# Two 8-block DMA transposes into two rings instead of one 16-block transpose into one ring, in a chunked linear-attention kernel with two feed-forward layers

## The chip, the cores and the metric

The program runs on one core of a Trainium2 chip. The metric is device time of one execution in microseconds (us); lower is better. Engines in the text: PE (TensorE, matrix products), DVE (VectorE), ACT (ScalarE), POOL (GpSimd) and SP (SyncE, which here only issues DMAs). Each engine works through its own list of instructions in order.

## The reference

A recurrent attention runs over 768 time steps for 4 batches of 8 heads, head size 40; its output goes through two feed-forward layers, the first with h·cos(h), the second with h·clip(h+3, 0, 6)/6.

```python
for t in range(S):                       # S = 768, state is (B, H, D, D), D = 40
    y[:, :, t] = einsum('bhd,bhde->bhe', r_t, state)
    Sa = einsum('bhde,bhe->bhd', state, a_t)
    state = state * w_t[:, :, None, :] - einsum('bhd,bhe->bhde', Sa, b_t)
    state = state + einsum('bhd,bhe->bhde', v_t, k_t)
x = y reshaped to (3072, 320)
h = x @ w_in;  x = (h * cos(h)) @ w_out                  # 320 -> 2048 -> 320
h = x @ w_in2; x = (h * clip(h + 3, 0, 6) / 6) @ w_out2
```

## The kernel before, in words

The 768 steps are cut into 12 chunks of 64 steps. A *unit* is one chunk of one batch (8 heads): 48 units, numbered n = 4·chunk + batch. Each unit's work comes in two parts.

*Preparation*, which doesn't need the state. `pA` loads the rows of a, r, b and k (tile `raw`) and the decays (`pip`). `pB` multiplies them and writes the k/b rows and the a/r rows as fp16 (the halves `KBss` and `ARss` of the tile `AKs`, two buffers in turn). `pT` turns both by a DMA transpose issued by SP. `pC` multiplies the turned rows on PE (tile `p`, 8 matmuls), masks the product on DVE (`LN`) and stores it for the inverse. For each chunk, `iL` to `iE` invert the triangular matrices of all four units; `iB` is a chain of 62 short DVE instructions (`tmp`, `Tt`).

*The recurrence*, in the order of the chunks: `cU` (PE products with the state, `uh`), `cA`, a transpose `FT` of the rows `FS`, `cG` (`gm`, `GF`), and `cF`, which ends the unit with the output `xy` and the new state. It reads the turned a/r rows (`ART`) up to its end.

The feed-forward work of a chunk is 8 *groups* a layer (`mA`, `mB`), 192 groups in all. A group is 16 PE matmuls into `h`, one ACT function and one DVE instruction that make `s`, a rounded copy `ghl` of `s` by ACT or DVE, the rest of the rounding by DVE (`ghl<-s,ghl`), and 12 matmuls into `acc`. `h` and `s` have two buffers each, `ghl` three.

No order is written by hand. Each operation is recorded by `Plan.rec` (from L156) with an assumed cost, and `Plan.order` (L244) lists them for the engines by 50 passes of a priority schedule over these costs and the data dependencies. An operation recorded as `either` goes to DVE, or for a copy to DVE or ACT, whichever the schedule finds free. So one edited operation, cost or buffer can move any instruction of any engine. The emitted instructions all carry the lines of `emit` (L452, L456), so the rows below go by tile.

The turned rows lie in `AKT` (L556), nine slots of 8 blocks. Unit n takes two neighbouring slots, n mod 8 and the one behind it (L846): a/r rows first, k/b rows second. Slot n mod 8 + 1 still holds the a/r rows of unit n-7, so the transpose of unit n waits for `cF` of unit n-7, and for `pC` of unit n-1, whose k/b rows are in the first slot.

Of the kernel before, what the change touches and what calls it, by code (L numbers as in the profile page):

```python
# [9 lines left out]
F16 = mybir.dt.float16  # L10
# [9 lines left out]
B, H, S, D = 4, 8, 768, 40  # L20
# [66 lines left out]
class Plan:  # L87
# [68 lines left out]
    def rec(self, attr, eng, name, a, kw):  # L156
        i = len(self.ops)
# [7 lines left out]
        n = max(_free(x) for x in outs[:1] + (ins if name in ("tensor_reduce", "activation") else []))  # L165
        dma = None
        if name.startswith("dma"):
            sb = outs[0] if outs[0].tensor.__class__.__name__ == "Tile" and outs[0].tensor._space != DRAM else ins[0]
            by = 1
            for k in outs[0].shape:  # L170
                by *= k
            by *= mybir.dt.size(outs[0].dtype)
            if name == "dma_start":
                run = _run(outs[0], ins[0])
                k = by // run
                c = 520.0 if k <= 64 else 640.0 if k <= 128 else 960.0 if sb.shape[0] == 40 else 740.0
                run = min(run, 20480)
                dma = by / run * (9 + run * 0.045) / 16
            else:
                r, w = ins[0].shape[0], by // 2 // ins[0].shape[0]  # L180
                dma = w / 128 * 204 * (1 if r >= 64 else r / 128)
                c = 1310.0 if w < 1024 else 1390.0 if w < 2048 else 1500.0
        elif eng == "PE":
            m = _free(ins[0])
            c = max(n / 2.4 + 2.5, 25.0 if m == 128 else 32.0)
            if ins[0].dtype == F32:
                c = 30.0 if m == 32 else max(2 * (5 + 0.835 * m), 4 * n / 2.4)
            shape = tuple(32 if x <= 32 else 64 if x <= 64 else 128 for x in (ins[0].shape[0], _free(ins[0])))
        elif eng in ("DVE", "ANY"):
            c = 70 + n * 1.042  # L190
            es = max(mybir.dt.size(x.dtype) for x in outs + ins)
            if name == "tensor_copy":
                c = 70 + n * (0.26 if es == 2 else 0.52)
            elif name == "tensor_tensor" and n > 512 and any(len(x.ap) > 2 and abs(x.ap[-1][0]) > 4 for x in ins):
                c = 70 + n * 1.906
            elif name == "tensor_scalar":
                c = 70 + n * 0.52
            elif name == "reciprocal":
                c = 70 + n * 6.3
            elif name == "tensor_tensor_scan":  # L200
                c = 70 + n * 2.08
            if any(_free(x) == 1 for x in ins):
                c += 60
        elif eng == "ACT":
            c = 95 + n * 0.833
            if "accum_out" in kw:
                c += 93
            elif "bias" in kw:
                c += 50
            elif ins[0].tensor._space == PSUM:  # L210
                c -= 42

        turn = name == "tensor_copy" and n > 512 and abs(outs[0].ap[-1][0]) > 4
        if turn:
            c = 70 + n * 1.906
        rate = 2.56 if any(abs(x.ap[-1][0]) > 4 for x in ins) else 2.1 if all(mybir.dt.size(x.dtype) == 4 for x in outs + ins) else 1.88
        cp = 36 + n * 0.83 if name == "memset" else 150 + n * (rate if name == "tensor_tensor" else 3.4)
        if eng == "POOL":
            c = cp
# [251 lines left out]
def _free(ap):  # L471
    n = 1
    for k in ap.shape[1:]:
        n *= k
    return n
# [10 lines left out]
def _run(o, i):  # L486

    run = 1
    a, b = list(o.ap), list(i.ap)
    if len(a) != len(b):  # L490
        a, b = a[-1:], b[-1:]
    for k in range(len(a) - 1, -1, -1):
        if a[k][0] != run or b[k][0] != run or (k == 0 and len(a) > 1):
            break
        run *= a[k][1]
    return run * mybir.dt.size(o.dtype)
# [3 lines left out]
def kernel(  # L500
# [20 lines left out]
    def pool(name, n, **k):  # L521
        return main.enter_context(tc.tile_pool(name=name, bufs=n, **k))

    big = pool("big", 1)
    p1 = Rings(big, 1)
    p2 = Rings(big, 2)
    p3 = Rings(big, 3)
    pE = Rings(big, 8)
    pN = Rings(big, 5)
    dr = pool("dr", 1, space=DRAM)  # L530
    ps = pool("ps", 1, space=PSUM)
# [20 lines left out]
        COL[nm] = (ncol, ncol + k)  # L552
        ncol += k
    acc = fl.tile([128, ncol], F32, name="acc")
    AKs = [big.tile([128, 2 * H, 128], F16, name=f"AKs{i}") for i in range(2)]
    AKT = big.tile([128, 9 * H, 128], F16, name="AKT")  # L556
    ARss, KBss = ([t[:, x * H:x * H + H] for t in AKs] for x in range(2))
    pip0 = big.tile([128, H, 2, D], F32, name="pip0")
    TTp = big.tile([128, NH * C + 64], F16, name="TT")
    TT = TTp[:, 0:NH * C].rearrange("p (h t) -> p h t", h=NH)  # L560
# [32 lines left out]
    tq = nc.sync  # L593
# [231 lines left out]
    ART_t = {}  # L825
    KBT_t = {}

    def pB(n):
        raw, pip = st_raw.pop(n)
        nc.either.tensor_copy(out=pip[64:128, :, 1], in_=pip[0:64, :, 1])  # L830
        rf = raw.rearrange("p h x e -> p (h x e)")
        nc.either.tensor_tensor(out=rf, in0=rf, in1=pip.rearrange("p h x e -> p (h x e)"), op=ALU.mult)
        kb, ar = KBss[n % 2], ARss[n % 2]
        kv = kb[:, :, 0:120].rearrange("p h (x e) -> p h x e", e=D)
        nc.either.tensor_copy(out=kv[:, :, 0::2, :], in_=bc2(raw[:, :, 1]))
        dp("kb", E_KB).tensor_tensor(out=kb[:, :, 40:80], in0=raw[:, :, 1], in1=kb[:, :, 0:40], op=ALU.subtract)
        av = ar[:, :, 0:80].rearrange("p h (x e) -> p h x e", e=D)
        nc.either.tensor_copy(out=av, in_=bc2(raw[:, :, 0]))
        dp("ar", E_AR).tensor_tensor(out=ar[:, :, 80:120], in0=raw[:, :, 0], in1=ar[:, :, 0:40], op=ALU.subtract)
        square(rf, 0, 128, 640, "raw", n, rf)  # L840
        E_t[n] = pE.tile([128, H, 2 * D], F16, tag="E", name="E")
        nc.either.tensor_copy(out=E_t[n], in_=kb[:, :, 0:2 * D])
        later(0.7, pT, n)

    def pT(n):
        t = AKT[:, n % 8 * H:n % 8 * H + 2 * H]  # L846
        ART_t[n], KBT_t[n] = t[:, 0:H], t[:, H:2 * H]
        tq.dma_start_transpose(out=t, in_=AKs[n % 2].rearrange("p h e -> p (h e)"))

    NT_t = {}  # L850

# [534 lines left out]
    for c in range(NC):  # L1386
        O = T_0 if c == 0 else 0
        t = 16 * c - T_P - O
        for b in range(B):
            n = c * B + b  # L1390
# [3 lines left out]
        t = 16 * c - T_I - O  # L1394
# [5 lines left out]
        t = t + D_I + 2.1  # L1400
        at(t, iD, c)
        at(t + 0.4, iE, c)
        t = 16 * c - T_C - O
        for b in range(B):
            n = c * B + b
# [17 lines left out]
    for m, (wi, wo) in enumerate(((moe_w_in, moe_w_out), (moe2_w_in, moe2_w_out))):  # L1423
        l = [(wi, "i", i) for i in range(12)] + [(wo, "o", i) for i in range(10)]
        w0, w1 = ((T_W0, T_W0E), (T_W1, T_W1E))[m]
        for i, (src, kind, k) in enumerate(l):
            t = w0 + (w1 - w0) * i / len(l)
# [78 lines left out]
```

## Time and profile before

| | us |
|---|---|
| median of 3 runs | 1154.57 (1153.92 to 1156.34) |
| the profiled execution | 1160.31 |
| its span, first to last instruction | 1158.5 |
| DVE busy | 1012.2 (87%) |
| PE busy | 854.8 (74%) |
| ACT busy | 829.1 (72%) |

The profiled execution is one run of its own, 5.74 us above the median. The busy shares are means over stretches that differ: PE has nothing to do at first and is nearly always busy from 354 us on; DVE is busy from 50 us to the end of the last unit.

### The profile page before, as it was taken

The numbers are of one execution on the slowest core, as the hardware profiler recorded it, in microseconds if no ns is written. First come the engines' busy times: TensorE is split into PE (matmuls) and PEld (weight loads), VectorE is DVE, ScalarE is ACT, GpSimd is POOL, SyncE is SP. The second block draws the span as 40 slices with busy tenths as digits, with TensorE's granted clock in tenths as the row PEclk, the third lists the DMA queues.
The fourth block names the chain that finished last, engine by engine and source line by source line (L and its number), as shares of the span: only waits on it lengthen the run. The fifth ranks groups of instructions, "written<-read, shape, count | busy, mean of one in ns | idle before, by whom it ended". The sixth has DMA issues, their size and how long they took to land. (4 is left out here: it accounts for less than half of the span.)

```text
span 1158.5 us, 29299 instructions
## 1 busy us (share of the span) xinstructions
PE 854.8 (74%) x11378; PEld 688.8 (59%) x11378; DVE 1012.2 (87%) x2379; ACT 829.1 (72%) x1736; POOL 19.4 (2%) x85
## 2 busy tenths in 40 slices
PE   0010122842859898998899998999989989999993
PEld 0000122741648777786777777777778868787872
DVE  7699999899999899998899998999879969999552
ACT  5575679997879887798876887858778747574241
POOL 2000000000000000000000000000000000000000
PEclk9999999975869899999999998999989999999997
DMA  6989867999947996669966588864885752621011
GB/s 208 242 173 275 191 145 163 243 235 185 216 97 156 160 182 125 126 129 168 173 126 128 109 161 162 148 134 92 139 154 122 131 121 61 111 51 33 1 26 15
DMA packets 475510, 162.61 MB, mean 140 GB/s; under 512 B 445637, under 2 KB 457969, under 8 KB 474978
## 3 DMA queue, kind: packets, MB, share of 16 engines
q1 hardware_dynamic: 475074, 159.99, 67.9%
q8 instruction: 91, 1.49, 0.6%
q10 hardware_dynamic: 288, 0.67, 0.2%
q14 instruction: 57, 0.47, 0.1%
HBM read 80.09 MB, written 25.61 MB: 91 GB/s over the span
## 5 line engine op out<-in xcount | busy, mean ns | idle before, releaser
L456 PE MATMUL acc<-wout,ghl 128*128 128x320 f16 x2304 | 359.8, 304 | 2.2 <-DVE ghl L456 1.6
L456 PEld LDWEIGHTS <-win 128*128 128x128 f16 x3328 | 311.7, 101 | 75.3 <-issue 31.7
L456 PEld LDWEIGHTS <-ghl 128*128 128x128 f16 x2304 | 216.7, 99 | 80.2 <-DVE ghl L456 3.0
L456 PE MATMUL h<-x1T,win 128*128 128x256 f16 (+1 forms) x1664 | 193.4, 275 | 21.3 <-DVE s L456 16.8
L456 ACT ACTIVATE s<-h,cvec 128x512 f32<-128x512 f32 x192 | 130.8, 682 | 105.7 <-PE h L456 68.7
L456 PE MATMUL h<-x2T,win 128*128 128x256 f16 (+1 forms) x1664 | 185.2, 267 | 6.2 <-DVE s L456 6.2
L456 PEld LDWEIGHTS <-AKT 120*128 120x128 f16 (+1 forms) x1088 | 63.0, 107 | 149.8 <-DMA AKT<-AKs 132.4
L456 DVE TENSOR_TENSOR ghl<-s,ghl 128x512 f16<-128x512 f32 x192 | 131.3, 685 | 3.9 <-ACT ghl L452 1.6
L456 PE MATMUL p<-AKT 120*128 120x64 f16 x384 | 22.3, 208 | 131.3 <-DMA AKT<-AKs 100.2
L452 ACT ACTIVATE ghl<-s 128x512 f16<-128x512 f32 x146 | 90.8, 623 | 25.2 <-DVE s L456 23.5
L456 DVE TENSOR_TENSOR tmp<-Tt,Lt 128x126 f32<-128x126 f32 (+22 forms) x372 | 92.7, 249 | 6.7 <-DMA Lt<-Ls 1.8
L456 DVE TENSOR_TENSOR Tt<-Tt,tmp 128x126 f32<-128x126 f32 (+22 forms) x372 | 92.4, 248 | 4.7
L456 DVE SCALAR_TENSOR_TENSOR s<-h,s 128x512 f32<-128x512 f32 x96 | 65.7, 685 | 21.0 <-ACT s L456 20.2
L456 DVE SCALAR_TENSOR_TENSOR s<-s,h 128x512 f32<-128x512 f32 x96 | 65.2, 680 | 18.5 <-ACT s L456 18.1
L456 PE MATMUL t<-E,GF 128*128 128x40 f16 x1152 | 46.1, 185 | 35.4 <-DVE GF L456 31.5
L456 PE MATMUL t<-FS,NT 128*128 128x40 f16 x768 | 37.6, 185 | 36.5 <-DVE FS L456 16.5
L456 PEld LDWEIGHTS <-GF 128*128 128x128 f16 x1152 | 38.2, 99 | 43.4 <-DVE GF L456 36.3
L456 PEld LDWEIGHTS <-NT 128*128 128x128 f16 x768 | 33.3, 100 | 38.2 <-issue 32.0
L452 ACT ACTIVATE AKs<-raw 128x640 f16<-128x640 f32 x67 | 47.2, 729 | 9.0 <-DVE raw L456 8.3
L456 PEld LDWEIGHTS <-TT 64*128 64x128 f16 (+1 forms) x768 | 27.7, 97 | 32.5 <-issue 23.0
L456 DVE TENSOR_TENSOR AKs<-raw,AKs 128x320 f16<-128x320 f32 x92 | 42.7, 483 | 1.4 <-ACT AKs L452 1.2
L456 DVE TENSOR_TENSOR raw<-raw,pip 128x640 f32<-128x640 f32 x46 | 37.7, 820 | 6.6 <-DMA raw<-in_arbk_dram 4.6
(138 smaller groups left out, 1458.0 us busy)
## 6 DMA issues: line engine op xcount, KB each, us to landing
raw<-in_arbk_dram SPq DMA_DIRECT2D x46, 320.0 KB
v<-in_vv_dram SPq DMA_DIRECT2D x48, 160.0 KB
pip<-Dec SPq DMA_DIRECT2D x46, 160.0 KB
wout<-in_moe_w_in_dram SPq DMA_DIRECT2D x12, 512.0 KB
Ls<-LN SPq DMA_DIRECT2D x48, 128.0 KB
Lt<-Ls SPq DMA_DIRECT2D x48, 128.0 KB
TT<-Thl SPq DMA_DIRECT2D x12, 512.0 KB
wout<-in_moe_w_out_dram SPq DMA_DIRECT2D x10, 512.0 KB
```

The lines of the kernel that those rows point to most:

```text
L452: self.nc.scalar.activation(func=AF.Copy, **kw)
L456: getattr(getattr(self.nc, attr), name)(*a, **kw)
```

## The change

The tile `AKs` becomes two tiles `KBs` and `ARs`, and `pT` issues two transposes of 8 blocks instead of one of 16. The k/b rows land in a single buffer (`KBT`), the a/r rows in a ring of eight (`ART`). The a/r rows of unit n now overwrite those of unit n-8, and the k/b rows overwrite only k/b rows. The assumed issue cost of a 16-block transpose (1500 ns) goes from the table of costs, and 8-block ones stay at 1390 ns each. Bytes, products and precision are as before.

```diff
-                c = 1310.0 if w < 1024 else 1390.0 if w < 2048 else 1500.0
+                c = 1390.0 if r == 128 and w >= 1024 else 1310.0
...
+    pA_ = Rings(big, 8)
...
-    AKs = [big.tile([128, 2 * H, 128], F16, name=f"AKs{i}") for i in range(2)]
-    AKT = big.tile([128, 9 * H, 128], F16, name="AKT")
-    ARss, KBss = ([t[:, x * H:x * H + H] for t in AKs] for x in range(2))
+    KBss = [big.tile([128, H, 128], F16, name=f"KBs{i}") for i in range(2)]
+    ARss = [big.tile([128, H, 128], F16, name=f"ARs{i}") for i in range(2)]
...
     def pT(n):
-        t = AKT[:, n % 8 * H:n % 8 * H + 2 * H]
-        ART_t[n], KBT_t[n] = t[:, 0:H], t[:, H:2 * H]
-        tq.dma_start_transpose(out=t, in_=AKs[n % 2].rearrange("p h e -> p (h e)"))
+        KBT_t[n] = p1.tile([128, H, 128], F16, tag="KBT", name="KBT")
+        ART_t[n] = pA_.tile([128, H, 128], F16, tag="ART", name="ART")
+        tq.dma_start_transpose(out=KBT_t[n], in_=KBss[n % 2].rearrange("p h e -> p (h e)"))
+        tq.dma_start_transpose(out=ART_t[n], in_=ARss[n % 2].rearrange("p h e -> p (h e)"))
```

The planner lists everything anew. Three places show it; a name ends in the number of its buffer, which differs between the two programs.

First, SP around the transpose of unit 11, the last of chunk 2. Before:

```order
L456 DMA_TRANSPOSE FT_130<-FS_82 128x8x128
L456 DMA wout_71<-in_moe_w_in_dram 64x1024
L456 DMA Ds<-raw_114 32x320
L456 DMA_TRANSPOSE AKT<-AKs_77 128x16x128
L456 DMA wstat<-in_moe_w_in_dram 128x1024
L456 DMA_TRANSPOSE x1T_95<-S8a 128x6x64
L456 DMA_TRANSPOSE FT_130<-FS_81 128x8x128
```

After:

```order
L456 DMA Srep_88<-Tt 40x16x40 x2
L456 DMA wout_70<-in_moe_w_out_dram 128x1024
L456 DMA_TRANSPOSE ART_128<-ARs_79 128x8x128
L456 DMA_TRANSPOSE x1T_95<-S8a 128x6x64
L456 DMA_TRANSPOSE KBT_124<-KBs_77 128x8x128
L456 DMA Ls_103<-LN_134 64x16x32
L456 DMA Srep_88<-Tt 40x16x40
L456 DMA Lt_92<-Ls_104 32x8x32 x4
```

It moved forward: on PE the product of unit 11 stood behind the 7th feed-forward group, and stands now ahead of the first.

Second, SP around the transpose of unit 18 (chunk 4). Before:

```order
L456 DMA Ls_102<-LN_124 64x16x32
L456 DMA raw_114<-in_arbk_dram 128x640
L456 DMA_TRANSPOSE AKT<-AKs_76 128x16x128
L456 DMA_TRANSPOSE x1T_94<-S8a 128x6x64
L456 DMA v_125<-in_vv_dram 64x2x320 x2
```

After:

```order
L456 DMA_TRANSPOSE KBT_124<-KBs_76 128x8x128
L456 DMA Tm_106<-Tt 64x16x32
L456 DMA raw_115<-in_arbk_dram 128x640
L456 DMA Thl_108<-Tt 64x16x32
L456 DMA Tm_106<-S8a 64x16x32
L456 DMA Thl_108<-Tt 64x16x32 x3
L456 DMA_TRANSPOSE ART_127<-ARs_78 128x8x128
```

Seven other DMAs stand between the two halves of one unit here. The halves are neighbours in 21 of the 48 units; in the other 27 between 1 and 11 DMAs stand between them, 1.8 a unit on the mean of all 48.

Third, DVE at the 115th feed-forward group (its `s` to its `ghl`). Before:

```order
L456 COPY S8a<-Tt 32x256
L456 TENSOR_TENSOR GF_84<-gm_132,GF_83 128x8x64
L456 TENSOR_TENSOR Tt<-Tt 128x512
L456 TENSOR_TENSOR S8a<-S8a,xy_133 40x320
L456 TENSOR_TENSOR Tt<-S8a,Tt 40x8x40
L456 TENSOR_TENSOR ghl_138<-s_136,ghl_138 128x512
```

After:

```order
L456 TENSOR_TENSOR gm_142<-t_138,mskG 128x512
L456 SCALAR_TENSOR_TENSOR s_147<-s_147,h_145 128x512
L456 CAST ghl_148<-s_146 128x512
L456 COPY GF_84<-FS_82 128x8x40
L456 TENSOR_TENSOR ghl_148<-s_146,ghl_148 128x512
```

The rounding copy (CAST) of this group went from ACT to DVE. Over the program DVE's copies of this kind go from 46 to 56.

## Rows read from the trace of the kernel before

**Rows 1.** The page's head: span, and busy time of each engine.

```profile
span 1158.5 us, 29299 instructions
PE 854.8 (74%) x11378; PEld 688.8 (59%) x11378; DVE 1012.2 (87%) x2379; ACT 829.1 (72%) x1736; POOL 19.4 (2%) x85
```

**Rows 2.** Busy time by stretch; cuts at feed-forward groups 1, 17, 49, 145, last unit.

```profile
core 0: us, PE busy (x) PEld busy (x) DVE busy (x) ACT busy (x) POOL busy (x), PEclk, DMA share, GB/s
0.00:50.00 50.00, 0.00 (x0) 0.00 (x0) 31.75 (x53) 25.94 (x41) 8.31 (x30) 1.00 0.79 232
50.00:213.40 163.40, 32.74 (x736) 28.59 (x737) 150.25 (x334) 119.07 (x234) 2.02 (x10) 1.00 0.87 194
213.40:353.90 140.50, 83.54 (x1230) 68.09 (x1230) 134.43 (x333) 118.07 (x248) 1.01 (x5) 0.76 0.83 188
353.90:504.10 150.20, 137.98 (x1911) 112.04 (x1910) 140.10 (x346) 124.03 (x267) 2.03 (x10) 0.97 0.78 145
504.10:950.30 446.20, 413.29 (x5415) 329.93 (x5414) 401.95 (x975) 341.02 (x732) 6.07 (x30) 0.97 0.74 139
950.30:1047.70 97.40, 95.11 (x1310) 77.66 (x1309) 94.12 (x219) 65.82 (x147) 0.00 (x0) 1.00 0.38 70
1047.70:1158.50 110.80, 92.15 (x784) 72.51 (x782) 59.60 (x127) 35.18 (x72) 0.00 (x0) 0.93 0.10 19
```

**Rows 3.** Waits of DVE, 350 to 1000 us: total, times, longest.

```profile
DVE s L456 <- ACT s L456: 13.0, 15, 2.4
DVE LN L456 <- DMA Ls<-LN: 5.4, 4, 3.3
```

**Rows 4.** Timeline: the last unit's output, the last products, the last instruction.

```profile
1047.69 0.54 DVE L456 SCALAR_TENSOR_TENSOR xy<-t,cvec,pd 64x320 f32<-64x320 f32 x1
...
1137.00 3.43 PE L456 MATMUL acc<-wout,ghl 128*128 128x320 f16 x24
...
1152.18 0.14 DVE L456 TENSOR_SCALAR bad<-Tt 1x1 int32<-1x1 f32 x1
```

**Rows 5.** The chain of waits: one feed-forward group's two runs on PE.

```profile
1062.20 1.75 PE h L456 x16
...
1068.55 1.63 PE acc L456 x12
```

**Rows 6.** SP's transposes by tile: shortest, median, longest ns; 16 blocks, 8 blocks.

```profile
L456 SPq DMA_TRANSPOSE AKT<-AKs x48: 1316/3024/6387, 55.1 to 923.0; - x48
L456 SPq DMA_TRANSPOSE FT<-FS x48: 1231/1270/1987, 144.8 to 1037.7; - x48
```

**Rows 7.** Waits of PE's weight loads for transposes, 350 to 1000 us.

```profile
PEld L456 <- DMA FT<-FS: 3.8, 5, 1.6
PEld L456 <- DMA AKT<-AKs: 2.9, 3, 1.2
```

**Rows 8.** Timeline: the end of unit 4's products and the transpose of unit 11.

```profile
227.81 0.57 PE L456 MATMUL t<-E,GF 128*128 128x40 f16 x16
227.96 3.26 SPq L456 DMA_TRANSPOSE AKT<-AKs  x1
```

**Rows 9.** DVE's copies by form: times, busy us, mean ns, idle before.

```profile
L456 DVE CAST ghl<-s 128x512 f16<-128x512 f32 x46 | 19.5, 424 | 5.6 <-PE acc L456 4.4
L456 DVE CAST AKs<-raw 128x640 f16<-128x640 f32 x25 | 12.1, 486 | 0.1
L456 DVE CAST GF<-gm 128x512 f16<-128x512 f32 x13 | 5.4, 416 | 0.0
L456 DVE CAST S8a<-xy 64x320 f16<-64x320 f32 x14 | 4.4, 314 | 0.7 <-DMA x1T<-S8a 0.6
L456 DVE CAST NT<-LN 64x512 f16<-64x512 f32 x5 | 2.1, 422 | 0.1
L456 DVE COPY uh<-uh 64x320 f16<-64x320 f16 x5 | 1.2, 238 | 0.2
```

**Rows 10.** The same rounding copy on ACT.

```profile
L452 ACT ACTIVATE ghl<-s 128x512 f16<-128x512 f32 x146 | 90.8, 623 | 25.2 <-DVE s L456 23.5
```

## The prediction

> **What bounds the kernel now.** I read the page's head first, for the span of 1158.5 us and the engine that is busiest, DVE with 1012.2 us [rows 1]. A mean over the span doesn't say whether that engine sets the time, so the second view is busy time by stretch, cut where the program's character changes [rows 2]. Up to the first feed-forward group (213 us) DVE prepares units and weights and PE is almost idle. From 213 to 354 us DVE is busy 134.4 of 140.5 us and PE 83.5. From 354 to 1048 us both are nearly full: in the long stretch from 504 to 950 us DVE has 44.3 us of idle time in 446.2, PE 32.9. After the last unit's output at 1047.7 us only feed-forward work is left, PE is busy 92.2 of 110.8 us and DVE about half. So there are two questions: when the last unit ends, which DVE sets with PE close behind, and how much feed-forward work is then left, which PE sets.
>
> The third view is the waits, to see what DVE's idle time is made of. In 350 to 1000 us it waited 13.0 us for ACT's `s` and 5.4 us for a DMA of `Ls`, its two largest [rows 3]; the rest are gaps too small to have a releaser. DVE is thus held up little by others, and its time is the number of its instructions times their length. The tail is the same either way: in the new order, as in the old, 25 of the 192 runs on `h` stand behind the last unit's product, and 28 before or 27 now of the 192 runs on `acc`. At 1.75 and 1.63 us each [rows 5] that is 89.4 us before; with the flags' reduction and the last output it is the 110.8 us of the last stretch, whose last products start at 1137.0 us and last instruction at 1152.2 us [rows 4]. One run on `acc` less is -1.6 us at the tail and as much ahead of it, so zero.
>
> **The change part by part.**
>
> *The transposes on SP.* Before, 48 with a median of 3.02 us; now 96 of the shape that `FT` has, median 1.27 us [rows 6]: 145.2 us of SP's time become 121.9. If the second of a pair finds the queue as full as a 16-block one does, the two take 3.0 us together and nothing is saved. So SP's time changes by -23 to 0 us. Almost none of it is on the path: from 350 to 1000 us PE's weight loads waited 2.9 us in all for `AKT` [rows 7]. I take 0; at best the 2.9 us go.
>
> Here a rule of the Trainium skill speaks against the change. SP held itself 3.02 us for 16 blocks and 1.27 us for 8 [rows 6]; by that row two small ones cost no more than a large one. The skill (DMA: Bandwidth & Descriptors, "Anatomy of one DMA — SWDGE (gpsimd) path") gives each DMA about 2.0 us that don't shrink with its size, most of it until the landing is confirmed; the section measures another issuing path than SP's, and no row here isolates that time. By it 48 more transposes would be 96 us of added waiting, if each were waited for. The waits of 2.9 us say that they are not, so the sum stays as it is by this rule too.
>
> *The added wait.* `pC` now waits for two landings, and in 27 units other DMAs stand between the two issues, 1.8 on the mean over all units, 11 at most. PE's product of that unit waits for the later one, and with it everything behind it in PE's order. The nearest row is `FT`, an 8-block transpose whose product follows at once: PE waited 3.8 us for it in 650 us [rows 7]. Bounds: 0 to +4 us there. I take 0, since a unit's preparation runs far ahead of its recurrence. If that cover were gone, 1.8 issues at the 1.27 us of a short transpose are 2.3 us for each unit that is waited for.
>
> *The ring.* Before, the transpose of unit 11 started at 227.96 us, right behind unit 4's last products, which started at 227.81 [rows 8]: the slot had just come free. Now it needs unit 3 only, and the new order puts it ahead of all feed-forward groups. That takes away a wait of SP and lets chunk 2's inverse start sooner, but the inverse is DVE's own work, and DVE is 96% busy from 213 to 354 us [rows 2]. A sooner start displaces other DVE work: 0 us by itself.
>
> *DVE's work.* This is the term that counts. The planner gave DVE more copies that ACT did before, and counted over the whole order the rows differ like this: `ghl` 46 to 56, at 0.424 us: +4.24; `S8a` from `xy` 14 to 20, at 0.314: +1.88; `NT` 5 to 9, at 0.422: +1.69; `uh` 5 to 9, at 0.238: +0.95; `GF` 13 to 15, at 0.416: +0.83; the copies into the k/b and a/r tiles 26 to 20, at 0.486: -2.92 [rows 9]. Ten smaller kinds net to -0.8. The sum is +5.9 us, on DVE, and all of the added `ghl` copies stand ahead of the last unit's end. Neighbouring DVE records overlap by up to 0.1 us (2379 records whose lengths add up to 1135 us have 1012.2 us busy), so 5.9 us of records are 5.9 × 0.89 = 5.3 us of time. ACT loses ten copies of 0.623 us [rows 10] and some smaller ones; it is idle 105 us in the long stretch [rows 2], so that gains 0. Bounds: 0, if all of it fits into DVE's idle time, and +5.9. I take +5.3, because DVE's idle time is small gaps and not waits.
>
> *The order.* I counted, with the mean of each form, how much DVE work stands ahead of each feed-forward group. Ahead of the 49th it is 28.0 us less than before, 25 us of time: the new order runs feed-forward work earlier and units later. From the 49th to the 145th group it is 433 us of time where it was 403, so that the two orders are within 8 us of each other from there on, and the lead is given back. Net 0 where DVE is the bound; this is the weak term of the sum, and both rivals are made of it.
>
> **Sum.** The profiled execution took 1160.31 us. Transposes 0, added wait 0, ring 0, DVE work +5.3, order 0, tail 0: 1165.6 us. The median of the runs is 5.74 us below the profiled execution, so 1159.9 us; I predict **1160 us**.
>
> **The rivals.**
>
> *Faster: the early lead is kept.* It works if DVE's idle time in the long stretch shrinks, so that the 30 us of work that come back there are partly absorbed. From 213 to 504 us DVE idled 16.2 us in 290.7, or 5.6%; from 504 to 950 us it idled 9.9% [rows 2]. At 5.6% that stretch has 25 us idle instead of 44.3: -19.3. With the +5.3: 1154.6 + 5.3 - 19.3 = 1140.6 us. For it: PE gets feed-forward work earlier, exactly where it is idle. Against it: DVE's idle time there was not waiting for feed-forward work to come.
>
> *Slower: the units are bunched.* Over chunks 4 to 9, 94 feed-forward groups began before between the first product with the state of a chunk and its last unit's end; in the new order 65 do. Units are DVE's work mostly, groups PE's. Taken in eights of groups from the 49th to the 144th, DVE's work was 28 to 42 us an eight, even beside PE's 28 to 40. Now it alternates, mostly 39 to 52 in one and 25 to 33 in the next. Where DVE has 48 and PE 38, PE waits; in the next eight PE's 29 is the limit and DVE waits. Adding the larger of the engines of each eight gives 425 us before and 441 now: +16, and the end at 1159.9 + 16 = 1176 us. It decides if PE and DVE can't run apart by the difference of 10 us in an eight; two buffers of `h` and `s` and three of `ghl` are two to three groups, 7 to 10 us at 3.4 us each [rows 5]. Against it: the same sum over the first 48 groups is smaller than before, and with the cuts of the eights moved by one to seven groups the difference over all 192 goes from -20 to +19 us.
>
> *Slower: the added wait counts at the start,* where nothing runs ahead yet. PE can't begin before the first chunk's four units are turned; four times 2 us is +8, with the DVE term 1168 us. Against it: DVE has 150 us of work in these 163 us [rows 2] and doesn't wait for PE.
>
> *Nothing is left.* The casts fall into gaps and the order cancels: 1154.6 us.
>
> **How the numbers follow.** A measurement of this kernel can tell a change of about 0.2%, 2.3 us, from none. My forecast has 0.40 (its own range 1154 to 1167), the kept lead 0.25, the bunching 0.25, the start 0.05, nothing left 0.05. Within 2.3 us of 1154.6 fall nothing left, a quarter of the forecast and a little of the others' edges: 0.17. Faster: the kept lead less its edge, and the forecast's lower edge: 0.25. Slower: the rest, 0.58. The kept lead's 1141 and the bunching's 1176 are middles of their cases; a range from 1145 to 1176 leaves out a part of both, some 2 in 10 together.
>
> **What would show it.** Right: DVE busy up by 4 to 6 us at a like span of its idle time, the 49th group earlier by some 20 us, the 145th at most 8 us off, a tail of 111 us. `AKT`'s median of 3.02 us becomes two of 1.3 and PE's waits for the turned rows stay under 7 us from 350 to 1000 us. Wrong for the kept lead's reason: DVE's idle time from the 49th to the 145th group under 30 us. Wrong for the bunching's: idle time there over 55 us for both engines. Wrong for the transposes' own reason: waits of PE or DVE for `KBT` or `ART` of 10 us or more after the first group.

## The result and the profile after

The changed kernel takes 1167.38 us (median of 4 runs, 1167.12 to 1168.21) where the kernel before took 1155.18 (4 runs, 1153.92 to 1156.34): ratio 1.0095, 95% interval [1.0068, 1.0123]. It is slower by 12.2 us at the medians. The profiled executions lie closer together, 1167.3 us after and 1160.31 before, so the two traces can account for 6.1 us of span. Of the other 6.1 us, 0.9 lie outside the span (2.7 us of the time after, 1.8 before; no view shows what they are), and 5.1 are that the profiled execution of before lies above the median of these four runs. It is an ordinary one beside the sets of the experiments below, where the kernel before has medians of 1159.2 to 1160.5 us.

The page's head of the changed kernel, as in [rows 1]:

```profile
span 1164.6 us, 29423 instructions
PE 855.3 (73%) x11378; PEld 688.4 (59%) x11378; DVE 1013.1 (87%) x2399; ACT 823.5 (71%) x1716; POOL 19.6 (2%) x85
```

DVE has 20 instructions more and 0.9 us more of busy time in a span 6.1 us longer. The time went into DVE's idle time, not into its work. Where, is seen in busy time by stretch, with cuts at the same five events as in [rows 2]:

```profile
core 0: us, PE busy (x) PEld busy (x) DVE busy (x) ACT busy (x) POOL busy (x), PEclk, DMA share, GB/s
0.00:50.00 50.00, 0.00 (x0) 0.00 (x0) 35.18 (x59) 29.24 (x46) 8.27 (x30) 1.00 0.81 236
50.00:221.00 171.00, 33.05 (x736) 28.28 (x737) 152.11 (x346) 122.17 (x232) 2.02 (x10) 1.00 0.90 199
221.00:335.30 114.30, 79.11 (x1116) 64.89 (x1116) 108.20 (x227) 105.79 (x231) 1.01 (x5) 0.78 0.89 193
335.30:486.70 151.40, 135.63 (x1850) 110.40 (x1850) 138.53 (x348) 114.67 (x247) 2.18 (x10) 0.97 0.71 137
486.70:955.00 468.30, 418.51 (x5586) 333.46 (x5585) 426.21 (x1075) 350.43 (x746) 6.08 (x30) 0.97 0.75 139
955.00:1054.50 99.50, 97.29 (x1313) 78.92 (x1312) 93.58 (x224) 66.27 (x148) 0.00 (x0) 0.98 0.38 69
1054.50:1164.60 110.10, 91.68 (x783) 72.40 (x781) 59.23 (x125) 34.88 (x71) 0.00 (x0) 0.93 0.10 19
```

Read the length of a stretch less DVE's busy time in it, and set it beside [rows 2]. Up to the 49th group (486.7 us, before 504.1) DVE has done 434.0 us of work instead of 456.5, in 17.4 us less: the lead that was counted is there. It idled 52.7 us where it had idled 47.6, 5.1 more. In the long stretch the 24.3 us of work come back and take 22.1 us of time, with 42.1 us of idle time where there were 44.3. The next stretch idles 5.9 us instead of 3.3, and the tail is as it was (110.1 us, 110.8). Up to the last unit's output DVE has 1.4 us more work and 5.6 us more idle time.

The waits of DVE from 350 to 1000 us, as in [rows 3], here the four largest after, then two of before that stand next to those of [rows 3]:

```profile
DVE TT L456 <- ACT TT L456: 10.0, 14, 2.4
DVE s L456 <- ACT s L456: 9.5, 13, 2.3
DVE gm L456 <- PE t L456: 4.8, 4, 1.9
DVE ghl L456 <- ACT ghl L452: 3.3, 7, 0.8
```

```profile
DVE raw L456 <- DMA raw<-in_arbk_dram: 4.6, 6, 2.7
DVE TT L456 <- ACT TT L456: 3.5, 6, 0.8
```

The same 650 us by busy time, before and after:

```profile
350.00:1000.00 650.00, 603.00 (x7982) 484.51 (x7980) 594.23 (x1458) 501.06 (x1078) 8.10 (x40) 0.97 0.72 135
```

```profile
350.00:1000.00 650.00, 586.16 (x7773) 469.29 (x7771) 594.11 (x1506) 483.19 (x1032) 8.26 (x40) 0.97 0.72 134
```

The waits of PE's weight loads for transposes, as in [rows 7]:

```profile
PEld L456 <- DMA FT<-FS: 9.5, 5, 2.5
PEld L456 <- DMA KBT<-KBs: 0.4, 1, 0.4
```

`TT <- ACT TT` is new among DVE's largest waits. `TT` is the end of the inverse (L946 and L947 of the kernel before): ACT rounds a product of PE into `TT`, DVE takes the remainder right behind it, four times for a chunk. It is not a loss by itself: DVE's idle time in this window is 55.9 us after and 55.8 before, and what `TT` adds (6.5 us), `LN` (5.4 to 0.5), `raw` (4.6 to 0.2) and `s` (13.0 to 9.5) give back. The turned rows themselves are waited for less than before; `FT`, which stands behind them on SP, more.

The transposes on SP by tile, shortest, median and longest in ns, as in [rows 6]:

```profile
L456 SPq DMA_TRANSPOSE KBT<-KBs x48: 1231/1270/3172, 58.9 to 934.6; - x48
L456 SPq DMA_TRANSPOSE ART<-ARs x48: 1231/1320/6751, 52.1 to 931.1; - x48
L456 SPq DMA_TRANSPOSE FT<-FS x48: 1231/1252/3004, 152.2 to 1042.7; - x48
```

At the medians a pair holds SP 2.6 us where one held it 3.0. But a few long ones weigh heavily: added up over all records, the pairs hold SP 149.7 us (1.47 and 1.65 us on the mean) and the 16-block ones held it 144.9 (3.02). SP's time was not saved. DVE's copies by form, as in [rows 9]:

```profile
L456 DVE CAST ghl<-s 128x512 f16<-128x512 f32 x56 | 23.7, 424 | 5.9 <-PE acc L456 4.5
L456 DVE CAST S8a<-xy 64x320 f16<-64x320 f32 x20 | 6.2, 312 | 0.1
L456 DVE CAST NT<-LN 64x512 f16<-64x512 f32 x9 | 3.8, 423 | 2.3 <-PE t L456 2.0
```

Counts and lengths are those of the prediction. The forms whose number changed come to +5.45 us of records, and all others to -2.78, a quarter of a per cent of their length. Before's profiled execution ran these a little slow: in three other kernels with its own 2379 instructions they are 3 us shorter in all, too.

### The profile page after: what moved, and what is told of

It is laid out like the page before. It is cut to its first block, busy times and chain, and to the rows that moved or that the text cites. A ratio compares the mean times of both kernels' runs of the same rounds, so it can differ in the third digit from the quotient of the medians.

```text
span 1164.6 us, 29423 instructions
## 1 busy us (share of the span) xinstructions
PE 855.3 (73%) x11378; PEld 688.4 (59%) x11378; DVE 1013.1 (87%) x2399; ACT 823.5 (71%) x1716; POOL 19.6 (2%) x85
## 5 line engine op out<-in xcount | busy, mean ns | idle before, releaser
L456 PE MATMUL h<-x1T,win 128*128 128x256 f16 (+1 forms) x1664 | 189.4, 272 | 15.5 <-DVE s L456 13.9
L456 PE MATMUL h<-x2T,win 128*128 128x256 f16 (+1 forms) x1664 | 188.6, 270 | 14.1 <-DVE s L456 12.5
L456 PE MATMUL p<-ART,KBT 120*128 120x64 f16 x384 | 21.9, 206 | 116.7 <-DMA KBT<-KBs 90.0
L452 ACT ACTIVATE ghl<-s 128x512 f16<-128x512 f32 x136 | 84.2, 623 | 23.5 <-DVE s L456 17.2
L456 PEld LDWEIGHTS <-KBT 120*128 120x128 f16 x384 | 18.6, 106 | 121.0 <-DMA KBT<-KBs 91.3
L456 PE MATMUL t<-E,GF 128*128 128x40 f16 x1152 | 45.8, 184 | 44.3 <-DVE GF L456 40.8
L456 PEld LDWEIGHTS <-ART 120*64 120x64 f16 (+1 forms) x704 | 43.9, 106 | 3.4 <-issue 1.1
L456 PE MATMUL q<-Lt 32*32 32x32 f32 x1536 | 22.1, 201 | 30.0 <-DMA Lt<-Tm 22.7
L456 DVE SCALAR_TENSOR_TENSOR wout<-wout 128x512 int32<-128x512 int32 (+1 forms) x56 | 37.9, 682 | 5.0 <-ACT wout L456 4.5
```

What stands on the lines that cost most here:

```text
L452: self.nc.scalar.activation(func=AF.Copy, **kw)
L456: getattr(getattr(self.nc, attr), name)(*a, **kw)
```

## The experiments

Three theories stood. *Work*: DVE's added copies are the time. *Transposes*: the second transpose, its landing or the rings are. *Order*: the new list of instructions lets DVE wait more, whatever was the occasion for it. All kernels were timed beside runs of the kernel before on the same chip; those runs had medians of 1159.2 to 1160.5 us and a wider scatter (some 1151 to 1166) than the first ones, so ratios are compared and not microseconds.

**1. The changed program in the old order.** `issue` takes a stored order and a stored engine for each copy instead of the planner's; `KBT` and `ART` are turned one right behind the other where `AKT` was.

```diff
     def issue(self):
-        for i in self.order():
+        order, on = json.loads(zlib.decompress(base64.b85decode(PLANNED)))
+        for o, e in zip(self.ops, on):
+            o["on"] = dict(P="PE", D="DVE", A="ACT", G="POOL", S="SP")[e]
+        for i in order:
             self.emit(i)
```

> The changed program (two transposes, two rings) with every instruction in the order and on the engine of the kernel before; the two transposes of a unit stand side by side where the one stood. If the shift comes from the new order or from the moved copies, this is the kernel before within 2 us: 1153 to 1158 us. If the two transposes themselves cost (issue, landing, the wait for two), it keeps a large part of the shift: 1160 to 1168 us.

1166.28 us, ratio 1.0063 [1.0038, 1.0088], with six runs in two groups (1159.6 and 1160.5; 1166.3 to 1168.5). Since the groups were not to be understood, it was run again:

> The changed program in the old order once more: its six runs fell into two groups, 1159.6 and 1160.5 us, and four of 1166 to 1168. If the transposes cost a fixed amount, ratio 1.006 again; if that was scatter between executions, 1.000 to 1.004. Its trace, if the profiled run falls in the upper group, says where the 7 us are.

1160.58 us, 12 runs, ratio 1.0010 [0.9987, 1.0034]. The same program gave 0.6% and 0.1%: the intervals that go with the ratios don't hold what differs from one set to the next, and half a per cent is about what can be told here. DVE's work up to the last unit's output in both, and in the changed kernel's second profile (experiment 3):

```profile
0.00:1046.23 1046.23, 761.79 (x10596) 615.96 (x10597) 952.36 (x2254) 793.39 (x1664) 19.44 (x85) 0.95 0.76 153
```

```profile
0.00:1041.68 1041.68, 757.85 (x10596) 613.90 (x10597) 952.02 (x2254) 794.68 (x1664) 19.49 (x85) 0.96 0.76 154
```

```profile
0.00:1055.36 1055.36, 764.82 (x10599) 614.75 (x10600) 954.33 (x2276) 788.52 (x1645) 19.42 (x85) 0.96 0.76 152
```

With 93.9 and 89.7 us of idle time the two transposes in the old order are at before's 95.1 or below; the new order has 101.0. These three executions are each the shortest of their sets (1159.56, 1155.22 and 1169.1 us, 5 to 7 us under the medians), so they compare with each other, but less well with before's, which is an ordinary one; and none shows the 1166 us of the upper group. As far as they show it, the transposes do not make the idle time.

**2. The split alone.** The kernel before with its order, tiles and ring; in `emit` each 16-block transpose becomes two.

```diff
+            elif name == "dma_start_transpose" and kw["out"].shape[1] == 2 * H and kw["out"].shape[2] == 128:
+                for x in (1, 0):
+                    getattr(getattr(self.nc, attr), name)(out=kw["out"][:, x * H:x * H + H],
+                                                          in_=kw["in_"][:, x * H * 128:(x + 1) * H * 128])
```

> The kernel before, with its order, its tiles and its one ring kept; only each 16-block transpose is issued as two 8-block ones, back to back. If the second transpose itself costs the time that the old-order run showed (ratio 1.006), this has the same ratio, 1.004 to 1.009, near 1166 us where the kernel before is at 1159. If the two rings and the two staging tiles made that time, or if it was scatter, this stands at the kernel before: 1154 to 1162 us, ratio 0.998 to 1.003.

1164.17 us, 12 runs, ratio 1.0037 [1.0008, 1.0067], between the two expectations. Together with the three numbers above, turning the rows in two pieces costs 0.1 to 0.6% in an order made for one, 1 to 7 us. The trace shows one wait that it could come from: PE's weight loads wait 8.2 us for `FT`, before 3.8 [rows 7], in the two runs of the old order 5.4 and 6.2. It is no sure sign of the split: a plan with one transpose has 7.7 (experiment 7, at 1400).

**3. The changed kernel again,** in one set with the split alone and the second run of the old order.

> The changed kernel unaltered, beside the same runs of the kernel before as the others of this set. If order is what remains over the old-order run, it stands above that one by 2 to 6 us (1167 to 1172 us, ratio 1.008 to 1.011); if the transposes are all of it, the two are alike (1164 to 1168).

1174.55 us, ratio 1.0125 [1.0094, 1.0156], above both expectations. In this set the same changed program stands at 1.0010 in the old order and at 1.0125 in the new: the order is 1.15% of 1160 us, 13 us. The first set gives less: 1.0063 in the old order, beside 1.0123 for the new one with 20 copies moved (experiment 4), which is 0.6% or 7 us; and 1.0063 beside the first measurement's 1.0095 would be 4 us. That the new order costs time is shown in both sets, with intervals that don't touch; how much of the shift it is, is not known better than this. Its profile repeats the changed kernel's: `TT` waited for 11.6 us, and the 1st, 17th, 49th and 145th group start within 3 us of where they did.

**4. Twenty copies from DVE to ACT in the new order, and from ACT to DVE in the old.** Kernels as in experiment 1 with the new and the old order; 20 of the `ghl` copies ahead of the last unit's end change their engine.

> The changed kernel in its own order, but 20 of DVE's rounding copies ghl<-s (0.424 us each, 8.5 us in all) go to ACT, spread over the units' time; DVE has then 2.6 us of records less than before the change. If DVE's amount of work sets the end, as predicted, it gives 1160 us (7.6 us less than 1167). If the order sets it, 1165 to 1170 us.

> The order of the kernel before in the changed program, and 20 of ACT's rounding copies ghl<-s moved to DVE: 8.5 us of records more on DVE. If DVE's amount of work sets the end, 7.6 us more than the run with the old order alone. If DVE's small gaps take it, within 2 us of that run.

The first: 1173.8 us, ratio 1.0123 [1.0094, 1.0152], where the unaltered changed kernel has 1.0095 and 1.0125, both in other sets: no gain beside either. The second: 1166.63, ratio 1.0061 [1.0033, 1.0090], where the old order without it had 1.0063 in the same set, but 1.0010 in the later one; beside that, the copies could have cost 0.5%. DVE's work up to the last unit's output, in this order:

```profile
0.00:1061.30 1061.30, 765.51 (x10597) 615.48 (x10598) 947.58 (x2255) 799.36 (x1665) 19.40 (x85) 0.95 0.76 151
```

```profile
0.00:1047.98 1047.98, 758.74 (x10596) 615.07 (x10597) 958.47 (x2272) 784.42 (x1645) 19.46 (x85) 0.96 0.76 153
```

Beside 954.33 and 952.36 above, the work went down by 6.8 and up by 6.1 us. The end came 5.9 us *later* in the first and 1.8 us later in the second; idle time took up the difference (113.7 and 89.5 us). In the old order the rows of DVE's waits from 350 to 1000 us add up to 38.3 us without the added copies and 34.7 with them: the waits took in much of the work. A copy that leaves one engine lands on the other, so ACT's work went up by 10.8 us in the first and down by 9.0 in the second; the planner's own change moved copies the same way as the second, from ACT to DVE. Work alone does not order the kernels either: 947.6 us of it end at 1061.3 here, and 958.2 us end at 1041.9 in experiment 7. So the theory of work falls as the account of the shift; that such copies cost nothing at all is not shown.

**5. Splices.** The old order up to the first feed-forward group and then what is left in the new; and the new order up to the 49th group and then what is left in the old.

```diff
+pre = first[:cut]
+order = pre + [i for i in second if i not in set(pre)]
```

> The changed program; everything that stood ahead of the first feed-forward group in the old order stands in that order, the rest in the new order. The new kernel is 7.9 us later at its first group. If the start sets the end, 1158 to 1161 us. If the middle (units bunched, DVE's gaps there) sets it, 1165 us or more; the first group is then earlier and the lead is lost again.

> The changed program: the new order up to the 49th feed-forward group, and from there what is left in the old order. If the new order's loss lies in what follows the 49th group (the lead given back), this keeps the lead of 17 us: 1145 to 1160 us. If it lies ahead of it (the later first group, the waits from 50 to 221 us), it stays at 1166 to 1174. The join itself may cost, as it did in the run with the old start (1192), and then it tells nothing.

1192.62 us (ratio 1.03 [1.027, 1.033]) and 1180.73 us (1.0183 [1.0147, 1.0219]), both slower than either whole order. The joins cost, and what each half is worth can't be read from the totals. The second one's stretches to the 17th group, to the 49th and to the 145th still say one thing:

```profile
0.00:337.80 337.80, 112.14 (x1852) 92.64 (x1853) 295.17 (x631) 256.93 (x506) 11.31 (x45) 0.92 0.87 201
337.80:522.60 184.80, 145.41 (x2022) 117.52 (x2022) 164.07 (x435) 130.50 (x282) 2.02 (x10) 0.89 0.69 129
522.60:966.60 444.00, 410.22 (x5417) 328.39 (x5415) 401.85 (x975) 341.14 (x732) 6.08 (x30) 0.98 0.74 140
```

At the 49th group, once the units that the old order has done by then are done too, it is at 522.6 us, 18.5 later than before, with 63.4 us of idle time against 47.6 and so 16 us more of waiting, 10.6 of them between the 17th and the 49th group, where the join is; from there it runs as before did (401.85 of 444.0 us). The lead of 17 us in groups is not there any more when the units have caught up.

**6. The order in the program with one transpose.** The kernel before, given the changed kernel's order; with one ring of nine slots its transpose can't stand where the two stood, and it was put where its buffers allow it.

> The kernel before, its one 16-block transpose and one ring kept, run in the changed kernel's order with that one's engine for every copy; the whole transpose stands where its ring lets it, which moves 208 of 2399 VectorE instructions by up to 47 places against the changed kernel. If the order is the cause, this is near the changed kernel without a second transpose: ratio 1.008 to 1.014 (1168 to 1176 us where the kernel before is at 1160). If the two transposes are, it is at the kernel before: 0.997 to 1.003.

1265.48 us, ratio 1.0910 [1.0871, 1.0949], which no theory had expected. PE's and DVE's longest waits here, from 350 to 1050 us:

```profile
PE p L620 <- DMA AKT<-AKs: 30.2, 10, 5.3
PE t L620 <- DVE FS L620: 22.5, 4, 12.8
```

```profile
DVE tmp L620 <- DMA Lt<-Ls: 23.7, 4, 7.0
DVE LN L620 <- PE p L620: 22.7, 5, 6.0
```

The turned rows come late, and the inverse's waits (`tmp`, `LN`) follow. As a test of the order alone it fails, since 208 DVE instructions had to move; what it shows is that the new order can't be had with one ring of nine slots: what comes nearest to it is 8% slower. Ring and order can't be priced apart.

**7. Other plans of both programs.** Only the planner's price for the transposes is changed: 2620 and 1400 ns for the one of the kernel before (1500), 750 ns for each of the two in the changed kernel.

```diff
-                c = 1310.0 if w < 1024 else 1390.0 if w < 2048 else 1500.0
+                c = 1310.0 if w < 1024 else 1390.0 if w < 2048 else 2620.0
```

> The kernel before with one 16-block transpose, the planner told 2620 ns for it instead of 1500 (what two cost in the changed kernel). Nothing but the order and the choice of engine for some copies differs from before. If order alone moves the time by some us whatever the reason of the new plan, this is 5 to 15 us off the kernel before, to either side; if the plan hardly matters and the transposes do, it is within 2 us of it.

> The kernel before, one transpose, the planner told 1400 ns for it instead of 1500: a change of price too small to mean anything. If a new plan is a draw, this is off the kernel before by some us to either side (1152 to 1170 us, outside 0.998 to 1.002 more likely than not). If plans are all alike unless something in them is wrong, it stays within 0.998 to 1.002.

> The changed kernel with its planner told 750 ns for each of the two transposes, so that a pair stands in the plan for the 1500 ns of the one before; another order comes out, the program and its tiles are the same. If the changed kernel's time is the luck of one plan, this lands elsewhere, 5 us or more away from it, most likely nearer to the kernel before: ratio 0.997 to 1.006. If the split, its waits or its ring cost under any plan, it is with the changed kernel: 1.009 to 1.015.

One transpose: 1155.65 us at 2620, ratio 0.9957 [0.9937, 0.9978]; 1162.42 at 1400, ratio 1.0020 [0.9992, 1.0048]. Two: 1170.27, ratio 1.0108 [1.0065, 1.0150]. The first is 4.8 us off the kernel before, just short of the 5 to 15 us that were expected of a draw; the second lies at the edge between its two expectations. By these ratios plans of one and the same program differ by up to 0.6%, little more than the 0.5% by which two sets of one order differed. The plan at 2620 has the lowest ratio of all, its interval clear of the kernel before. DVE up to its last unit's output, and in the other plan of two transposes:

```profile
0.00:1041.93 1041.93, 754.70 (x10596) 612.53 (x10597) 958.18 (x2258) 794.96 (x1666) 19.44 (x85) 0.96 0.76 154
```

```profile
0.00:1058.45 1058.45, 764.83 (x10599) 618.55 (x10600) 958.98 (x2279) 791.89 (x1654) 19.41 (x85) 0.95 0.75 152
```

DVE's work is the same to 0.8 us; the idle time is 83.7 and 99.5 us. But the hope that another plan would bring two transposes near to the kernel before was not met: both of their plans are 1% slower, the other two with one transpose within 0.5% of it.

**Where the new order waits.** The waits of DVE for `TT`, 350 to 1000 us: 3.5 us in the kernel before; 4.6 and 4.9 with two transposes in the old order, 4.2 with the split alone, 3.6 in both re-plans with one; 10.0 and 11.6 in the changed kernel, 13.0 with 20 copies less on DVE, 6.8 in the other plan of two; and 10.2 with one transpose in the nearest to the new order (experiment 6). It goes with the order, not with the transposes. The chunk with the longest of these waits, at 794 us in the changed kernel, on ACT and DVE (start, length, what; in brackets the idle time before and its releaser):

```profile
792.88 0.77 ACT L456 ACTIVATE TT<-q 32x256 f16<-32x256 f32 x2 [2.49 <-PE q L456]
793.68 0.42 DVE L456 SCALAR_TENSOR_TENSOR TT<-q,TT 32x256 f16<-32x256 f32 x1 [2.37 <-ACT TT L456]
794.13 0.38 ACT L456 ACTIVATE TT<-q 32x256 f16<-32x256 f32 x1 [0.48 <-DVE TT L456]
794.54 0.42 DVE L456 SCALAR_TENSOR_TENSOR TT<-q,TT 32x256 f16<-32x256 f32 x1 [0.44 <-ACT TT L456]
794.99 0.38 ACT L456 ACTIVATE TT<-q 32x256 f16<-32x256 f32 x1 [0.49 <-DVE TT L456]
795.40 0.86 DVE L456 SCALAR_TENSOR_TENSOR TT<-q,TT 32x256 f16<-32x256 f32 x2 [0.44 <-ACT TT L456]
```

DVE's four stand one behind the other, and three of them wait for ACT, 3.3 us in all. Most of it, 2.4 us, stands ahead of the first, and there ACT itself had just waited 2.5 us for PE's `q`, the inverse's last product: ACT is only the last link. In the old order the same chunk's four are spread over 9.2 us with other work between, and DVE idles 0.4 us on them. That deferred units come due together, with nothing left to put in front of such a wait, fits this; no run shows it, and `TT` is a mark of the new order rather than the sum of its loss (the other plan of two has 99.5 us of idle time with 6.8 on `TT`).

## Why the prediction came out as it did

Slower was right and 1167 us lies in the range, but the reason given for it was not the reason: that the number came near is luck.

- *DVE's work, +5.3, with "DVE's idle time is small gaps and not waits":* the step that failed. The view behind it was read wrongly: [rows 3] are two of its 16 rows, and the others are no gaps without a releaser. All 16 add up to 41.4 us, of 55.8 us of idle time in that window. So DVE was held up by others, and its time was not the number of its instructions times their length. The copies came as counted (+5.45 us of records), but busy time rose by 0.9 where 4 to 6 were named as the sign, and the idle time up to the last unit's output by 5.6. Experiment 4 shows that copies moved off DVE brought nothing.
- *The order, 0:* the weak term, put at nothing because DVE's work was the bound; by experiments 1, 3 and 4 it is the larger part of the time, 7 to 13 us in pairs of one set. The lead came as counted (the 49th group 17 us earlier by time) and was given back (the 145th 4.9 us late). The rival of the bunching is not borne out: 16 us were worked out for the long stretch, but idle time there is 42.1 us for DVE, less than before, and 49.8 for PE, and not over 55. Its sum also counted work that had only moved: by the prediction's own numbers DVE's work alone goes up by 30 us in these groups (403 to 433), and the 25 us of lead ahead of them were not taken off. The 5.6 us stand mostly elsewhere, 5.1 ahead of the 49th group and 2.6 behind the 145th. Only beside the old order in the same set does the long stretch idle more, 44.6 us against 39.7, old order first:

```profile
503.20:944.30 441.10, 410.43 (x5415) 328.36 (x5414) 401.38 (x975) 341.65 (x732) 6.09 (x30) 0.98 0.75 141
```

```profile
484.50:954.90 470.40, 420.09 (x5577) 333.37 (x5575) 425.79 (x1073) 349.49 (x745) 6.09 (x30) 0.97 0.75 138
```

  The kept lead (under 30 us there) is refuted for this order; it is what the re-plan at 2620 shows, 432.0 - 403.0 = 29.0 us of idle time from its 49th group to its 145th, without any early lead:

```profile
508.00:940.00 432.00, 405.80 (x5398) 326.74 (x5395) 403.04 (x979) 341.67 (x732) 6.07 (x30) 0.99 0.77 143
```

- *The transposes, 0 of -23 to 0, and the added wait, 0 of 0 to +4:* right for the turned rows themselves, whose waits fell from 2.9 to 0.4 us. The -23 came from a median times a count; the records add up to 4.8 us more than before, not less. `FT`, which stands behind them, went from 3.8 to 9.5. By experiments 1 and 2 these two terms are +1 to +7 us together, near the bound of +4, and not below nothing.
- *The ring, 0:* not as a wait of SP, but it isn't nothing: by experiment 6 the new order can't be had without its freedom.
- *The start, +8:* DVE's idle time up to the first group is 33.7 us after and 31.4 before by the stretches, 2 us more, and 31.5 in the second profile of the changed kernel. The first group starts 7.9 us later for the most part because 5.3 us more of DVE's work stand ahead of it. Not the cause.
- *The tail, 0:* right, 110.1 and 110.8 us.
- *The median below the profiled execution by 5.74:* this was carried over to the changed kernel, whose profiled execution lies at its median (1167.3 and 1167.38 us). Of the miss of 7.4 us 5.7 are here; against its own profiled time the sum of 1165.6 missed by 1.7, with the wrong term in it. The three runs behind the 5.74 were short ones, and the 0.2% that a measurement was said to tell was too little: sets of the kernel before have medians from 1154.57 to 1160.49 us.

Open: whether any plan of two transposes would be as good as the best of one. Two draws against three suggest that the freer ring leads this planner to defer units, but two are few, and ring and order were not separated.

## What to carry to other kernels

Where a planner writes the order, an edit is two changes: price the edit in the old order and the new order by itself, and expect the second to move the time by half a per cent or a whole one. Before an engine that is 90% busy is called bound by its work, add up all rows of its waits: here they were three quarters of its idle time, and copies of a few us vanished in them. A saving worked out from medians needs the sum beside it. A lead in one kind of work is worth nothing until the other kind has caught up: compare the times at which both are done.

## What the runs showed of the hardware

A 16-block transpose holds SP for no fixed time: shortest, median and longest 1316, 3024 and 6387 ns in the kernel before [rows 6], but in the slower kernel of experiment 6:

```profile
L620 SPq DMA_TRANSPOSE AKT<-AKs x48: 1687/2006/8100, 53.7 to 1033.9; - x48
```

An 8-block one (`FT`, `KBT`, `ART`) kept its median between 1246 and 1338 ns in every trace, while its longest went from 1945 to 7001. In sum the two kinds cost nearly the same: turning all 48 units held SP 144.9 to 149.3 us with one transpose each (129.6 in the slower kernel) and 146.6 to 151.6 us with two. What in the queue decides the length of one, no run here isolated. And one program with a fixed order, on one chip, gave 1155.2 to 1168.5 us in its 18 runs.
